# Expert weights laid out in runs of 4096 bytes, and the third weight set asked for by ScalarE behind its copy of the first gathered tokens

## The chip, the cores and the metric

The kernel runs on one core of a Trainium2 chip, as one program and one launch. The metric is the device time in microseconds (us) of one execution. Beside the times there is one profiled execution, whose trace gives every row shown below. Engines are named as in the profile: PE is TensorE (PEld its weight loads), DVE VectorE, ACT ScalarE, POOL GpSimd, SP SyncE. A "q" behind a name (SPq, ACTq) is that engine's sequencer, which also issues DMAs.

## The reference

Windowed attention (batch 8, 8 heads, 576 positions, head size 64) gives 4608 tokens of 512 numbers. A mixture of experts with a capacity follows: each token goes to the expert with the highest logit, each of the 8 experts keeps the 80 tokens of the highest gate weight, and all other rows of the output are zero.

```python
logits = x @ w_gate                                   # x: 4608 x 512 from the attention
expert_idx = np.argmax(logits, axis=1)
gate_w = probs[np.arange(N), expert_idx]
for e in range(8):
    tok_idx = ...                                     # of expert e, at most 80, highest gate_w
    h = np.maximum(x[tok_idx] @ w1[e], 0.0)           # w1[e]: 512 x 1024
    out[tok_idx] = gate_w[tok_idx, None] * (h @ w2[e])  # w2[e]: 1024 x 512
```

Each w1[e] and each w2[e] is 2 MB of float32, so one expert's set is 4 MB and all eight are 32 MB.

## The kernel before, in words

The first part, up to about 199 us, computes attention tile by tile (36 tiles of 128 tokens), writes the tokens to a DRAM buffer `x_dram`, fills the output with zeros, and works out which 80 tokens each expert keeps. The order of its instructions is a list of numbers written out by hand (`ORDER`, played by `play`). In it SP also loads the weight set of expert 0, in eight pieces of 512 KB (`first_weights`).

The second part is the experts. There are three buffers for weight sets in SBUF (`w_sets`), and expert e uses buffer e modulo 3. `weights(e)` asks for w1[e] and then w2[e] with one DMA of 2 MB each. SP asks for sets 1 and 2 at the end of the first part, and for set e+3 inside the loop once expert e has read its buffer: w1 when the last product of `ffn1(e)` is done, w2 when DVE has taken its last piece in `split(e)`.

For each expert the steps are:

- `gather(e)`: POOL issues an indirect DMA that fetches the 80 kept rows (160 KB) from `x_dram` into `xg`. All eight are issued one after the other at the start of the second part.
- `load_x(e)`: PE transposes `xg` into `tp`, and ACT copies it to `xgT` (for expert 0 ACT one half and DVE the other).
- `split(e)`: in four pieces, ACT rounds w2[e] to `wh` and DVE computes the rest `wl = w2 - wh`.
- `ffn1(e, 0)` and `ffn1(e, 4)`: PE multiplies w1[e] with `xgT` into `hp`, 64 products each; DVE turns each half into `hh` and `hl`.
- `ffn2(e)`: PE adds up three products for each of eight pieces (`hh` by `wh`, `hh` by `wl`, `hl` by `wh`) into `yp`; DVE scales the result to `y`, and POOL scatters `y` into the output with an indirect DMA.

The instructions of an engine run in the order written. For each expert the loop writes `load_x(e+1)`, `split(e+1)`, `weights(e+3)`, `ffn2(e)`, `ffn1(e+1, 0)`, `ffn1(e+1, 4)`. So on DVE the four `wl` of expert e+1 stand ahead of `y` of expert e, and that `y` stands ahead of `hh` and `hl` of expert e+1. Ahead of the first `load_x`, PE runs 24 products on idle data (L790). DMAs issued by SP are on queue q1, those by ACT on q10, and POOL's indirect ones on q0; all use the same 16 DMA engines.

Of the kernel before, what the change touches and what calls it, by code (L numbers as in the profile page):

```python
# [47 lines left out]
P = 128  # L48
# [55 lines left out]
def play(jobs, order):  # L104

    said, blocked = set(), {}
    ready = [False] * len(jobs)

    def advance(n):
        for r in jobs[n]:  # L110
            if not isinstance(r, str):
                if r[0] != "lat":
                    ready[n] = True
                    return
            elif r[0] == "!":
                said.add(r[1:])
                for m in blocked.pop(r[1:], ()):
                    advance(m)
            elif r[0] == "?" and r[1:] not in said:
                blocked.setdefault(r[1:], []).append(n)  # L120
                return

    for n in range(len(jobs)):
        advance(n)
    for n in order:
        assert ready[n], n
        ready[n] = False
        advance(n)
# [3 lines left out]
def attn_moe(ctx: ExitStack, tc: tile.TileContext, qk, v, w_gate, w1, w2, out, *, capacity, blocks, dbg=None):  # L132
    nc = tc.nc
# [3 lines left out]
    N, DM = out.shape  # L137
    E, F = w1.shape[0], w1.shape[3]
# [3 lines left out]
    KD = DM // P  # L142
# [88 lines left out]
    wp = ctx.enter_context(tc.tile_pool(name="wp", bufs=1))  # L231
    w_sets = [(wp.tile([P, KD, F], F32, name=f"w1_{i}"), wp.tile([P, KF, DM], F32, name=f"w2_{i}")) for i in range(3)]

    def weights(e):
        nc.sync.dma_start(w_sets[e % 3][0], w1[e])
        nc.sync.dma_start(w_sets[e % 3][1], w2[e])

    with ExitStack() as actx:
        ring = actx.enter_context(tc.tile_pool(name="ring", bufs=1))
# [131 lines left out]
        def first_weights(i):  # L371
            yield f"?spill{WEIGHTS_AT[i]}"
            yield "dma", 1.9
            e, i = i // NW, i % NW
            if i < KD:
                nc.sync.dma_start(w_sets[e][0][:, i], w1[e, :, i])
            else:
                c = 2 * (i - KD)
                nc.sync.dma_start(w_sets[e][1][:, c:c + 2], w2[e, :, c:c + 2])

        def tail(T):

# [302 lines left out]
        for i in range(len(WEIGHTS_AT)):  # L685
            jobs.append((2 * WEIGHTS_AT[i] + 3, first_weights(i)))
        for bi, made in enumerate(batches):
            for gi in made:
                t1 = sum(groups[gi]) - 1
# [21 lines left out]
        jobs.append((-1000, warm(False)))  # L711
        with tc.manual_schedule():
            play([gen for _, gen in jobs], ORDER)
            for e in range(1, 3):
                weights(e)

# [10 lines left out]
    def gather(e):  # L729
        xg = fk.tile([n_, DM], F32, name="xg", bufs=E)  # L730
        nc.gpsimd.indirect_dma_start(out=xg, out_offset=None, in_=x_dram[:, :],
                                     in_offset=bass.IndirectOffsetOnAxis(ap=src_i[:, e:e + 1], axis=0))
        xgs[e] = xg

    def split(e, f0, f1):
        if f0 == 0:
            wsp[e] = (wr.tile([P, KF, DM], F32R, name="wh"), wr.tile([P, KF, DM], F32R, name="wl"))
        wh, wl = wsp[e]
        for f in range(f0, f1, 2):
            nc.scalar.copy(wh[:, f:f + 2, :], w_sets[e % 3][1][:, f:f + 2, :])  # L740
            nc.vector.tensor_tensor(wl[:, f:f + 2, :], w_sets[e % 3][1][:, f:f + 2, :], wh[:, f:f + 2, :].bitcast(F32),  # L741
                                    op=ALU.subtract)

    def load_x(e):
        xTs[e] = fk.tile([P, KD, n_], F32, name="xgT")

        m = KD if e else KD // 2
        for c0 in range(0, KD, m):
            tp = ps_x.tile([P, KD, n_], F32, name="tp")
            for c in range(c0, c0 + m):  # L750
                nc.tensor.transpose(tp[:, c, :], xgs[e][:, P * c:P * (c + 1)], ident[0:n_, 0:n_])  # L751
            (nc.vector.tensor_copy if c0 else nc.scalar.copy)(xTs[e][:, c0:c0 + m], tp[:, c0:c0 + m])  # L752

    def ffn1(e, f0):
        if f0 == 0:
            hs[e] = (fk.tile([P, KF, n_], F32R, name="hh"), fk.tile([P, KF, n_], F32R, name="hl"))
        hh, hl = hs[e]
        hp = ps_h.tile([P, 4, n_], F32, name="hp")
        for f in range(4):
            for c in range(KD):  # L760
                for m in range(2):
                    col = P * (f0 + f) + 64 * m
                    nc.tensor.matmul(hp[64 * m:64 * m + 64, f, :], w_sets[e % 3][0][:, c, col:col + 64], xTs[e][:, c, :],  # L763
                                     start=(c == 0), stop=(c == KD - 1), tile_position=(0, 64 * m))
        nc.vector.tensor_scalar(hh[:, f0:f0 + 4, :], hp, 0.0, None, op0=ALU.max)
        nc.vector.scalar_tensor_tensor(hl[:, f0:f0 + 4, :], hp, 0.0, hh[:, f0:f0 + 4, :].bitcast(F32),
                                       op0=ALU.max, op1=ALU.subtract)

    def ffn2(e):
        hh, hl = hs[e]  # L770
        wh, wl = wsp[e]
        y = fk.tile([n_, DM], F32, name="y")

        w = DM if e + 1 < E else DM // 2
        for c in range(0, DM, w):
            yp = ps_y.tile([n_, DM], F32, name="yp")
            for f in range(KF):
                for i, (a, b) in enumerate(((hh, wh), (hh, wl), (hl, wh))):
                    nc.tensor.matmul(yp[:, 0:w], a[:, f, :], b[:, f, c:c + w], start=(f == 0 and i == 0),  # L779
                                     stop=(f == KF - 1 and i == 2))  # L780
            nc.vector.tensor_scalar(y[:, c:c + w], yp[:, 0:w], gw[:, e:e + 1], None, op0=ALU.mult)  # L781
        nc.gpsimd.indirect_dma_start(out=out[:, :], out_offset=bass.IndirectOffsetOnAxis(ap=dst_i[:, e:e + 1], axis=0),  # L782
                                     in_=y, in_offset=None, bounds_check=N - 1, oob_is_err=False)

    with tc.manual_schedule():
        for e in range(E):
            gather(e)
        t = ps_w.tile([P, 512], F32, name="warm")
        for _ in range(WARM2):
            nc.tensor.matmul(t[:, 0:WARMN], late, idle, start=True, stop=True)  # L790
        load_x(0)
        split(0, 0, 4)
        ffn1(0, 0)
        split(0, 4, KF)
        ffn1(0, 4)
        for e in range(E):
            if e + 1 < E:
                load_x(e + 1)
                split(e + 1, 0, KF)
            if e + 3 < E:  # L800
                weights(e + 3)
            ffn2(e)
            if e + 1 < E:
                ffn1(e + 1, 0)
                ffn1(e + 1, 4)
# [33 lines left out]
```

## Time and profile before

| | |
|---|---|
| time, median of 3 runs | 304.52 us (304.14 to 305.18) |
| profiled execution: time | 302.68 us |
| profiled execution: span, first to last instruction | 301.0 us |
| PE busy | 263.4 us, 88% of the span |
| DVE busy | 212.2 us, 71% |
| ACT busy | 140.1 us, 47% |
| moved by DMA | 84.41 MB, mean 280 GB/s |

The profiled execution took 1.84 us less than the median of the runs. Between its span and its time lie 1.68 us. A busy share is a mean over both parts, which have different limits, so the second part has to be looked at by itself.

### The profile page before, as it was taken

Reading aid. Unit: us, or ns where it says so; the run is one execution under the profiler, and the core shown is the slowest. Engines: PE = TensorE matmul, PEld = TensorE weight load, DVE = VectorE, ACT = ScalarE, POOL = GpSimd, SP = SyncE. Lnnn points to the kernel's source line nnn. Section 1 sums busy time; section 2 is a strip of 40 time slices with the busy share of each in tenths; the row PEclk is TensorE's granted clock in tenths of the full one; section 3 lists DMA queues with packets and bytes.
Section 4 is the critical chain, followed back from the end, with each engine's and each line's share of the span. In section 5 each row is a group of like instructions: output and inputs, shape, how many; then the busy total and the mean of one; then the engine's idle time right before and its main releaser. Section 6 shows DMA issues by size and latency. Waiting matters only on the chain. (4 is left out here: it accounts for less than half of the span.)

```text
span 301.0 us, 12891 instructions
## 1 busy us (share of the span) xinstructions
PE 263.4 (88%) x5616; PEld 213.2 (71%) x5616; DVE 212.2 (71%) x544; ACT 140.1 (47%) x300; POOL 137.6 (46%) x190
## 2 busy tenths in 40 slices
PE   8498899598999988979889988772999999999993
PEld 5387678486788777758877766562976887787693
DVE  0586776357889978977889999940876587667651
ACT  1475565355668565545647535101535235515500
POOL 5488577653779499636877640036010110110011
PEclk9999999879999999999999999997799999999999
DMA  7689786495877998998787849999999999998100
GB/s 266 245 294 317 226 278 168 161 283 178 277 254 240 297 302 283 307 342 285 238 286 195 311 138 301 359 435 352 334 333 365 425 433 425 425 421 356 39 24 22
DMA packets 26281, 84.41 MB, mean 280 GB/s; under 512 B 3057, under 2 KB 4209, under 8 KB 24433
## 3 DMA queue, kind: packets, MB, share of 16 engines
q1 hardware_dynamic: 25056, 80.90, 76.3%
q0 software_dynamic: 1024, 2.62, 2.6%
q8 instruction: 44, 0.72, 1.0%
q14 instruction: 13, 0.10, 0.1%
q10 hardware_dynamic: 144, 0.07, 0.1%
HBM read 63.39 MB, written 20.19 MB: 278 GB/s over the span
## 5 line engine op out<-in xcount | busy, mean ns | idle before, releaser
L285 PE MATMUL sc<-qkT 64*64 64x128 f32 x1152 | 43.7, 282 | 12.5 <-issue 8.5
L351 POOL TENSOR_TENSOR pL<-pL,keeps 128x512 f32<-128x512 f32 x36 | 45.9, 1279 | 15.3 <-ACT pL L329 12.6
L316 POOL TENSOR_TENSOR fd<-fd,mx 128x512 f32<-128x512 f32 x36 | 37.7, 1051 | 21.0 <-DVE mx L314 13.4
L285 PEld LDWEIGHTS sc<-qkT 64*64 64x64 f32 x1152 | 33.4, 137 | 19.5 <-issue 13.0
L741 DVE TENSOR_TENSOR wl<-w,wh 128x1024 fp32r<-128x1024 f32 x32 | 37.1, 1219 | 11.0 <-ACT wh L740 10.2
L782 POOL DMA_INDIRECT out_dram<-y,dst_i x8 | 7.4, 921 | 81.0 <-DVE y L781 81.0
L310 DVE COPY_PREDICATED fd<-mine,sc 128x512 f32<-128x512 int32 x36 | 26.5, 735 | 24.4 <-ACT fd L308 24.2
L401 PE MATMUL o<-vw,pL 64*64 64x65 f32 x1152 | 38.5, 225 | 2.7 <-issue 2.0
L763 PEld LDWEIGHTS hp<-xgT,w 128*64 128x64 f32 x1024 | 38.3, 143 | 3.1 <-issue 1.6
L763 PE MATMUL hp<-xgT,w 128*64 128x80 f32 x1024 | 39.6, 241 | 0.2 <-ACT xgT L752 0.2
L401 PE MATMUL o<-vw,pU 64*64 64x65 f32 x1024 | 37.2, 219 | 1.0 <-issue 1.0
L401 PEld LDWEIGHTS o<-vw,pL 64*64 64x64 f32 x1152 | 32.2, 134 | 7.7 <-issue 6.4
L308 ACT COPY fd<-sc 128x512 f32<-128x512 f32 (+1 forms) x36 | 21.1, 585 | 35.3 <-PE sc L285 35.2
L740 ACT CAST wh<-w 128x1024 fp32r<-128x1024 f32 x32 | 31.2, 1047 | 4.4 <-DMA w<-in_w_dram 4.3
L401 PEld LDWEIGHTS o<-vw,pU 64*64 64x64 f32 x1024 | 31.4, 135 | 1.4 <-issue 1.3
L752 ACT COPY xgT<-tp 128x320 f32<-128x320 f32 (+1 forms) x8 | 3.3, 410 | 51.7 <-PE tp L751 45.3
L779 PE MATMUL yp<-wh,hh 128*80 128x512 f32 (+1 forms) x72 | 26.8, 372 | 0.0
L779 PE MATMUL yp<-wl,hh 128*80 128x512 f32 (+1 forms) x72 | 26.4, 367 | 0.0
L779 PE MATMUL yp<-wh,hl 128*80 128x512 f32 (+1 forms) x72 | 26.3, 365 | 0.0
L422 PE MATMUL xT_ps<-ident,xt 128*128 128x128 f32 x144 | 23.4, 284 | 3.1 <-issue 1.7
L426 ACT COPY xT<-xT_ps 128x512 f32<-128x512 f32 x36 | 21.0, 587 | 9.6 <-PE xT_ps L422 8.9
L412 DVE TENSOR_TENSOR xt<-o,r 128x512 f32<-128x512 f32 x36 | 24.7, 686 | 0.9 <-DVE r L410 0.2
(117 smaller groups left out, 492.1 us busy)
## 6 DMA issues: line engine op xcount, KB each, us to landing
w<-in_w_dram SPq DMA_DIRECT2D x14, 2048.0 KB, 17.9
qkT<-in_qk_dram SPq DMA_DIRECT2D x32, 512.0 KB, 4.6
x_dram<-xt SPq DMA_DIRECT2D x36, 256.0 KB, 3.5
out_dram<-zeros SPq DMA_DIRECT2D x36, 256.0 KB, 4.7
vw<-in_v_dram SPq DMA_DIRECT2D x32, 260.0 KB, 4.7
w<-in_w_dram SPq DMA_DIRECT2D x8, 512.0 KB, 5.8
qkT<-in_qk_dram SPq DMA_DIRECT2D x8, 256.0 KB, 5.0
vw<-in_v_dram SPq DMA_DIRECT2D x8, 130.0 KB, 5.1
```

The lines of the kernel that those rows point to most:

```text
L285: nc.tensor.matmul(scs[T][64 * m:64 * m + 64, r, pr, :], qkT[hp, i, pr, 0, :], kw, start=True, stop=True, tile_position=(64 * r, 64 * m))
L308: nc.scalar.copy(fd[rows], sc[rows, :, :, 0:64])
L310: nc.vector.copy_predicated(fd, mine.unsqueeze(1).unsqueeze(1).broadcast_to([P, NP, 2, 64]), sc[:, :, :, 64:128])
L316: nc.gpsimd.tensor_tensor(fd, fd, mx.unsqueeze(3).broadcast_to([P, NP, 2, 64]), op=ALU.subtract)
L351: nc.gpsimd.tensor_tensor(pL, pL, keeps[:, 1:2, :].broadcast_to([P, 2 * NP, 64]), op=ALU.mult)
L401: nc.tensor.matmul(ov[64 * m:64 * m + 64, g, pr, :], pTs[T][1 - old][hp, 2 * pr + m, :], vw[hp, i - old, pr, :], start=(old == 0), stop=bo ...
L412: nc.vector.tensor_tensor(xt.rearrange("x a g d -> x g a d"), ov[:, :, :, 0:D], r.unsqueeze(3).broadcast_to([P, 2, 4, D]), op=ALU.mult)
L422: nc.tensor.transpose(tp[:, c, :], xf[:, P * c:P * (c + 1)], ident)
L740: nc.scalar.copy(wh[:, f:f + 2, :], w_sets[e % 3][1][:, f:f + 2, :])
L741: nc.vector.tensor_tensor(wl[:, f:f + 2, :], w_sets[e % 3][1][:, f:f + 2, :], wh[:, f:f + 2, :].bitcast(F32), op=ALU.subtract)
L763: nc.tensor.matmul(hp[64 * m:64 * m + 64, f, :], w_sets[e % 3][0][:, c, col:col + 64], xTs[e][:, c, :], start=(c == 0), stop=(c == KD - 1) ...
L779: nc.tensor.matmul(yp[:, 0:w], a[:, f, :], b[:, f, c:c + w], start=(f == 0 and i == 0), stop=(f == KF - 1 and i == 2))
```

## The change

The weights lie in DRAM in another order. Before, the 16 KB that one SBUF partition takes from w1[e] (or w2[e]) were contiguous, so that a 2 MB DMA was 128 runs of 16 KB. Now the array is cut in four blocks of 512 KB, and each block has 4 KB for each partition; a 2 MB DMA is 512 runs of 4 KB. The pieces of set 0, each one such block, had runs of 4 KB before and have them now, and lie contiguous as a whole. What stands in SBUF at the end is the same.

`weights` takes the engine that issues. SP asks for set 1 alone at the end of the first part. Set 2 is asked for by ACT, between `load_x(0)` and `split(0)`.

```diff
-    def weights(e):
-        nc.sync.dma_start(w_sets[e % 3][0], w1[e])
-        nc.sync.dma_start(w_sets[e % 3][1], w2[e])
+    def weights(e, eng=nc.sync):
+        t1, t2 = w_sets[e % 3]
+        eng.dma_start(t1, w1[e].rearrange("k p f -> p k f"))
+        eng.dma_start(t2.rearrange("p (k j) d -> p k j d", j=2), w2[e].rearrange("k p j d -> p k j d"))
...
             if i < KD:
-                nc.sync.dma_start(w_sets[e][0][:, i], w1[e, :, i])
+                nc.sync.dma_start(w_sets[e][0][:, i], w1[e, i])
             else:
                 c = 2 * (i - KD)
-                nc.sync.dma_start(w_sets[e][1][:, c:c + 2], w2[e, :, c:c + 2])
+                nc.sync.dma_start(w_sets[e][1][:, c:c + 2], w2[e, i - KD])
...
             play([gen for _, gen in jobs], ORDER)
-            for e in range(1, 3):
-                weights(e)
+            weights(1)
...
         load_x(0)
+        weights(2, nc.scalar)
         split(0, 0, 4)
...
-        "w1": inputs["moe_w1"].reshape(E, DM // P, P, F).transpose(0, 2, 1, 3),
-        "w2": inputs["moe_w2"].reshape(E, F // P, P, DM).transpose(0, 2, 1, 3),
+        "w1": inputs["moe_w1"].reshape(E, DM // P, P, F),
+        "w2": inputs["moe_w2"].reshape(E, F // P // 2, 2, P, DM).transpose(0, 1, 3, 2, 4),
```

On SP's queue, at the end of the first part, these instructions stood before (`w_0`, `w_1`, `w_2` are the three buffers, the numbers behind them the tile's own):

```order
L369 DMA out_dram<-zeros 128x512 x5
L235 DMA w_1_113<-in_w_dram 128x4096
L236 DMA w_1_114<-in_w_dram 128x4096
L235 DMA w_2_115<-in_w_dram 128x4096
L236 DMA w_2_116<-in_w_dram 128x4096
L235 DMA w_0_111<-in_w_dram 128x4096
L236 DMA w_0_112<-in_w_dram 128x4096
```

In the change the same place reads:

```order
L370 DMA out_dram<-zeros 128x512 x5
L236 DMA w_1_113<-in_w_dram 128x4x1024
L237 DMA w_1_114<-in_w_dram 128x4x1024
L236 DMA w_0_111<-in_w_dram 128x4x1024
L237 DMA w_0_112<-in_w_dram 128x4x1024
```

The two DMAs into buffer 2 are gone from SP, and set 3 (into buffer 0) follows set 1 there.

On ACT, where the second part begins with the copy of the first tokens, there stood before:

```order
L665 COPY wide_0_105<-vp 24x80
L555 COPY wide_2_101<-zt 24x384
L558 COPY wide_2_104<-zt 24x384
L665 COPY wide_1_106<-vp 24x80
L752 COPY xgT<-tp 128x160
L740 CAST wh<-w_0_112 128x1024 x4
```

Now there stand:

```order
L666 COPY wide_0_105<-vp 24x80
L556 COPY wide_2_101<-zt 24x384
L559 COPY wide_2_104<-zt 24x384
L666 COPY wide_1_106<-vp 24x80
L752 COPY xgT<-tp 128x160
L236 DMA w_2_115<-in_w_dram 128x4x1024
L237 DMA w_2_116<-in_w_dram 128x4x1024
L740 CAST wh<-w_0_112 128x1024 x4
```

The two DMAs stand between the copy of expert 0's tokens and the four casts of w2[0].

## Rows read from the trace of the kernel before

**Rows 1.** Page, part 2: DMA rate in 40 equal slices of the span.
```profile
GB/s 266 245 294 317 226 278 168 161 283 178 277 254 240 297 302 283 307 342 285 238 286 195 311 138 301 359 435 352 334 333 365 425 433 425 425 421 356 39 24 22
```

**Rows 2.** Waits from 190 us on: who, for whom, us in total, times, longest.
```profile
PE tp L751 <- DMA xg<-x_dram,src_i: 6.7, 1, 6.7
ACT wh L740 <- DMA w<-in_w_dram: 4.3, 5, 1.3
```

**Rows 3.** Timeline from 199 us: start, us, engine, line, operation, count, idle before.
```profile
199.25 2.79 PE L790 MATMUL warm<-idle,late 128*128 128x256 bf16 x24 [0.24 <-DVE late L586]
199.76 1.16 POOL L731 DMA_INDIRECT xg<-x_dram,src_i  x1 [23.06 <-DMA out_dram<-zeros]
...
209.35 0.29 ACT L752 COPY xgT<-tp 128x160 f32<-128x160 f32 x1 [14.31 <-PE tp L751]
209.61 3.88 ACT L740 CAST wh<-w 128x1024 fp32r<-128x1024 f32 x4
...
209.70 6.80 PE L763 MATMUL hp<-xgT,w 128*64 128x80 f32 x128 [0.16 <-ACT xgT L752]
```

**Rows 4.** Windows: busy of PE, PEld, DVE, ACT, POOL; clock, DMA share, GB/s.
```profile
3.70:4.20 0.50, 0.50 (x4) 0.38 (x3) 0.00 (x0) 0.00 (x0) 0.50 (x2) 1.00 1.03 426
206.00:208.00 2.00, 0.00 (x0) 0.00 (x0) 0.00 (x0) 0.00 (x0) 1.62 (x2) 0.85 0.98 332
214.00:216.00 2.00, 2.00 (x60) 2.00 (x58) 1.69 (x3) 0.00 (x0) 0.00 (x0) 0.94 1.08 323
196.00:204.00 8.00, 5.45 (x55) 4.26 (x53) 2.98 (x15) 0.00 (x0) 3.32 (x4) 1.00 1.05 437
206.00:228.00 22.00, 19.10 (x295) 16.26 (x296) 13.88 (x18) 8.79 (x11) 3.68 (x4) 0.84 1.01 333
232.00:274.00 42.00, 42.00 (x625) 32.94 (x624) 28.40 (x37) 16.68 (x20) 3.67 (x4) 1.00 1.01 426
```

**Rows 5.** DMA landings after issue: gathers and scatters (min/median/max), and w1[2].
```profile
DMA to landing us min/median/max: 8.9/16.5/23.8
...
DMA to landing us min/median/max: 2.6/7.6/10.5
...
w<-in_w_dram SPq DMA_DIRECT2D x1, 2048.0 KB, 23.9
```

**Rows 6.** DMA queues from 207 to 209 us, then 2 to 3: packets, MB, share.
```profile
q1 hardware_dynamic: 42, 0.54, 83.8%
q0 software_dynamic: 42, 0.12, 19.0%
...
q1 hardware_dynamic: 91, 0.19, 69.1%
q10 hardware_dynamic: 86, 0.04, 15.2%
```

**Rows 7.** Timeline of SP: issues of w1[1] and w1[2].
```profile
193.53 0.88 SPq L235 DMA_DIRECT2D w<-in_w_dram  x1
...
197.32 0.33 SPq L235 DMA_DIRECT2D w<-in_w_dram  x1
```

**Rows 8.** Timelines of ACT, DVE and PE around experts 0 and 1.
```profile
217.29 3.90 ACT L740 CAST wh<-w 128x1024 fp32r<-128x1024 f32 x4
228.82 3.90 ACT L740 CAST wh<-w 128x1024 fp32r<-128x1024 f32 x4 [0.82 <-DMA w<-in_w_dram]
...
218.41 4.62 DVE L741 TENSOR_TENSOR wl<-w,wh 128x1024 fp32r<-128x1024 f32 x4
222.95 0.74 DVE L781 TENSOR_SCALAR y<-yp,gw 80x512 f32<-80x512 f32 x1
225.41 0.49 DVE L765 TENSOR_SCALAR hh<-hp 128x320 fp32r<-128x320 f32 x1 [1.73 <-PE hp L763]
...
227.29 0.44 PE L779 MATMUL yp<-wh,hh 128*80 128x512 f32 x1
...
232.94 4.68 PE L763 MATMUL hp<-xgT,w 128*64 128x80 f32 x128
```

## Prediction

> **What bounds the kernel now.** I read the page first. Its slices of 7.5 us show the DMA rate rise to 435 GB/s where the experts begin, sink to 333 to 365 for four slices, and hold 421 to 433 for five more [rows 1]. So the experts have to be read apart from the attention, and with the DMA queues beside PE.
>
> The waits from 190 us on come next. Only two matter: PE waited 6.7 us for the first gathered tokens, and ACT waited five times, 4.3 us in all, for a w2 that was still on its way [rows 2]. The timeline shows the first wait. The 24 idle products of PE run from 199.25 to 202.04; the gather is issued at 199.76; ACT copies the transposed tokens at 209.35, and PE starts `ffn1(0)` at 209.70 [rows 3]. The gather landed 8.9 us after its issue; a scatter later in the run landed in 2.6 us at best [rows 5]. The queues show why it is slow: between 207 and 209 us q1 carries 42 packets and 0.54 MB, q0 also 42 packets but 0.12 MB [rows 6]. The two queues take turns packet by packet, and a packet of q1 is 16 KB (semaphore writes are counted too).
>
> The idle time costs PE its clock as well. The granted clock is 0.85 in the mean from 206 to 208, so it fell from 2.4 to 1.2 GHz at about 207.4, in PE's wait for the tokens; from 214 to 216 it is 0.94, so it came back at about 214.2 [rows 4]. `ffn1(0)` took 6.80 us [rows 3]; the same 128 products take 4.68 us at the full clock [rows 8], so the low clock cost 2.1 us.
>
> From expert 1 on PE is busy all the time and DMA is full too, 426 GB/s at a share of 1.01 [rows 4]. The two are close to equal: PE takes 5.65 us for `ffn2` (227.29 to 232.94) and 4.68 us for `ffn1` [rows 8], 10.3 us an expert, and a set of 4.19 MB with a scatter of 0.16 MB takes 10.2 us at 426 GB/s.
>
> **The change, part by part.**
>
> *The gather.* With 4 KB packets on q1 it waits for a quarter of the bytes at each turn. Bounds: 2.6 us (an idle DMA) and 8.9 us (nothing gained). Of the 6.3 us between, I keep a quarter: 2.6 + 1.6 = 4.2 us, so it lands at 204.0. PE's transposes, ACT's copy and DVE's half take about 1.0 us (208.7 to 209.70), so `ffn1(0)` starts at 205.0. PE has then waited 2 us, not 6.7, so I take the clock to stay at 2.4 GHz, and `ffn1(0)` ends at 209.7 instead of 216.5: a gain of 6.8 us at this place.
>
> *Set 2 on ACT.* ACT reaches its two issues at 204.9. An issue takes 0.33 to 0.88 us [rows 7]; at 0.4 each the casts of w2[0] start 0.8 us later than they could, 205.7. That delays `wl` of expert 0. DVE needs 4 x 1.16 us for `wl` (4.62 for four) and 2 x 1.0 us for `hh` and `hl`, so `ffn2(0)` starts at about 210.1, when its first `hl` is there, and ends at 216.2, and `ffn1(1)` ends at 220.9. With 0.88 for each issue it is 1 us more; the next step hides it, since w2[1] comes later still.
>
> *Where set 2 lands on the path.* This decides. At 205.3, when w2[2] has been asked for, w2[1] is not there. Before, w1[2] landed at 197.32 + 23.9 = 221.2 [rows 5, 7]. It was directly behind w2[1] on q1, and 2.1 MB at 333 GB/s [rows 4] take 6.3 us, so w2[1] landed at about 215, hidden, since ACT cast it only at 217.29 [rows 8]. In the change q10 carries set 2 beside it. At 2 to 3 us the trace has these two queues at once: 91 packets of q1 and 86 of q10 [rows 6], turn by turn. I allow 1.2 us from the issue to set 2's first packets (an estimate, under half of the 2.6 us in which the fastest scatter landed [rows 5]): 206.5. Then 8.5 us of w2[1]'s way are left, of which q1 has about 84% [rows 6], 7.1 us, and the gathers 1.4. With a q10 packet of equal size in each turn the 7.1 become 14.2: landing at 222.1. If the rate is 426 and not 333, as before and behind this stretch, everything shrinks by 426/333 = 1.28, to 12.2 us: 218.7. I take 221, nearer the slow end, since gathers are under way in most of the stretch and the slow rate came with them.
>
> The Trainium skill says the same of such queues ("DMA: Bandwidth & Descriptors", section "Queues, rings and completion order"): each DMA engine takes turns between its queue rows, packet by packet. By its section "Issuing engines are not separate DMA queues", issuing from more engines saves only issue time and the transfers interleave. The trace agrees, with 91 packets against 86. By these sections asking from ACT brings no bandwidth, and takes half of the rate from whatever SP has under way; the sum by them is the one below.
>
> *What w2[1] holds up.* Let it land at T. ACT casts, and DVE ends the four `wl` of expert 1 5.7 us later (217.29 to 223.03). Behind them on DVE stand `y` of expert 0, 0.74 us, and `hh` and `hl` of expert 1, 0.98 for the first pair [rows 8]. So `ffn2(1)` starts at T + 7.4 and ends 5.65 later, at T + 13.0. Before it ended at 232.94, set by PE. The point from which the new wait costs time is T = 219.9. With T = 221 it ends at 234.0, 1.1 us later than before.
>
> *The clock once more.* PE ends `ffn1(1)` at 220.9 and waits for `ffn2(1)` until 228.4, 7.5 us. The wait in which the clock fell before was 6.7 us, so I expect the same here, and for `ffn2(1)` the price that `ffn1(0)` paid, 2.1 us. Bounds: nothing, and half of the 5.5 us that the clock stayed low after work began (208.7 to 214.2), 2.7 us. Together: 1.1 + 2.1 = 3.2 us late.
>
> *The rest.* Experts 2 to 7 go on at PE's pace of 10.3 us, as before. The runs of 4 KB cost DMA a little: 426 GB/s at a share of 1.03 in a stretch with such packets alone, 437 at 1.05 for 16 KB and some of 2 KB, 426 at 1.01 for 16 KB later [rows 4]. At a full share that is 414 against 416 to 422, so up to 2%, 0.2 us a set or 1.4 for seven. Nothing at the end: PE comes 3.2 us later, and each set has that much more time. The pieces of set 0 keep their 4 KB packets, so the attention stays as it is.
>
> **Sum.** The gain of 6.8 us is used up before `ffn2(1)`, and 3.2 us are lost behind it: span 301.0 + 3.2 = 304.2 us, time 302.7 + 3.2 = 305.9. That execution was 1.8 us under the median of the runs, so the median comes to 304.5 + 3.2 = 307.7 us.
>
> **The rivals.**
>
> *Faster: w2[1] isn't held up.* If T stays under 215, because q1's packets go first or because w2[1] is almost down when q10 starts, the gain stays until the weights bind. ACT already waits up to 1.3 us for w2 [rows 2], so DMA would be the bound. The slow stretch would end with the gathers at about 214 instead of 228: 14 us at 333 instead of 426 are 3.1 us. 1.4 us go to the smaller packets, and about 1 us of slack in the last sets is used: 3.1 - 1.4 + 1 = 2.7 us faster, 301.8. Against it stands the even count of the two queues [rows 6]. 20%.
>
> *No change.* T near 219.9 and a clock that doesn't fall: at T = 218.7, PE waits from 220.9 to 226.1, 5.2 us, less than the 6.7 us of before, and `ffn2(1)` ends at 231.7. Then set 2, which shares its way with w1[3], is late by about as much. Within 1 us of before. 10%.
>
> *Slower by more.* The slow rate isn't tied to the gathers and holds until 228, as before: T = 222.1 or later by a larger share of gathers, say 224: `ffn2(1)` ends at 237.0 + 2.1 = 239.1, 6.2 us late, 310.7. 25%.
>
> *The gather is no sooner.* It waits for something other than packet size and lands at 208.7 again. Set 2 is then asked for at 210, 5 us of w2[1] are left at 211.2, and they double: T = 221, but PE ends `ffn1(1)` later, at about 226.5, and keeps its clock in `ffn2(1)`: 1.1 us slower, 305.6. 10%.
>
> **How the numbers follow.** My forecast, w2[1] at 219.9 to 223 and a fallen clock, has 35%, and 307.7 us is its time, 306.6 to 310.3 by its own bounds (T = 219.9 with 2.1 us for the clock, T = 223 with 2.7). The cases of less time on one side and more on the other give the range: 302.3 to 311.5. A measurement of this kernel can tell about 0.3%, 0.9 us. Faster 20%; within 0.3% the case of no change, 10%; slower 35 + 25 + 10 = 70%.
>
> **What would show it.** The first gather lands about 4 us after its issue and `ffn1(0)` takes 4.7 us at clock 1.00. ACT's casts of w2[1] wait for a DMA until about 221 (before 217.29 with no such wait). PE then has a gap of some 7 us ahead of `ffn2(1)`, and the windows show a clock under 1.00 behind it. Expert 1's `y` comes about 3 us later than before, and that distance stays to the end. It is wrong if ACT doesn't wait for w2[1], if set 2 lands behind set 1 as on one queue, or if q1 slows in the attention.

## The result, and the profile after

With the change the kernel takes 307.96 us (median of 4 runs, 307.38 to 315.02), and the kernel before on the same chip 304.85 us (median of 4, 304.14 to 310.44). The ratio is 1.0111, with a 95% interval from 1.0076 to 1.0146; disturbed executions are left out of it and of the ratios further down, but not of the medians. So the change is slower by about 1.1%. The profiled execution took 307.38 us, its span is 305.7 us.

Of the 4.7 us by which the span grew (301.0 to 305.7), 0.7 lie ahead of the second part: PE's idle products start at 199.97 us and not at 199.25 [rows 3]. Below, moments in the second part are counted from that start, so that runs can be laid over each other.

| us after the first idle product | before | change | difference |
|---|---|---|---|
| `ffn1(0)` starts | 10.45 | 7.57 | -2.9 |
| `ffn2(1)` starts | 28.0 | 25.15 | -2.9 |
| `ffn2(2)` starts | 38.6 | 40.63 | +2.0 |
| `ffn1(3)` starts | 44.2 | 48.16 | +3.9 |
| end | 101.75 | 105.73 | +4.0 |

In the kernel before, `ffn2(2)` and the `ffn1(3)` behind it stood here:

```profile
237.85 0.44 PE L779 MATMUL yp<-wh,hh 128*80 128x512 f32 x1
...
243.49 4.71 PE L763 MATMUL hp<-xgT,w 128*64 128x80 f32 x128
```

The gain is there, it is kept for two experts, and about 7 us are lost around `ffn2(2)`. The timeline of PE in the change shows it (start, us, engine, line, operation, count, idle time before it and its releaser):

```profile
199.97 2.79 PE L790 MATMUL warm<-idle,late 128*128 128x256 bf16 x24 [0.24 <-DVE late L587]
206.75 0.50 PE L751 MATMUL tp<-ident,xg 80*128 80x80 f32 x4 [3.99 <-DMA xg<-x_dram,src_i]
207.54 3.23 PE L763 MATMUL hp<-xgT,w 128*64 128x80 f32 x45 [0.29 <-ACT xgT L752]
211.17 3.12 PE L763 MATMUL hp<-xgT,w 128*64 128x80 f32 x83 [0.41 <-issue]
...
225.12 0.43 PE L779 MATMUL yp<-wh,hh 128*80 128x512 f32 x1
...
230.78 4.65 PE L763 MATMUL hp<-xgT,w 128*64 128x80 f32 x128
235.36 0.50 PE L751 MATMUL tp<-ident,xg 80*128 80x80 f32 x4
240.60 0.68 PE L779 MATMUL yp<-wh,hh 128*80 128x512 f32 x1 [4.74 <-DVE hh L765]
...
248.13 4.65 PE L763 MATMUL hp<-xgT,w 128*64 128x80 f32 x128
```

The wait for the first gathered tokens is down from 6.7 us [rows 2] to 3.99, since the first gather lands 6.2 us after its issue and not 8.9 [rows 5]:

```profile
DMA to landing us min/median/max: 6.2/8.7/8.9
```

`ffn2(1)` at 225.12 has no wait in front. `ffn2(2)` at 240.60 has 4.74 us, and takes 7.53 us up to 248.13 where 5.65 was usual [rows 8]. Its releaser is DVE's `hh`, so the wait is followed back to DVE and ACT. The timeline of ACT:

```profile
207.19 0.29 ACT L752 COPY xgT<-tp 128x160 f32<-128x160 f32 x1 [11.43 <-PE tp L751]
207.22 0.38 ACTq L236 DMA_DIRECT2D w<-in_w_dram  x1
207.64 0.52 ACTq L237 DMA_DIRECT2D w<-in_w_dram  x1
208.41 3.89 ACT L740 CAST wh<-w 128x1024 fp32r<-128x1024 f32 x4 [0.93 <-issue]
...
215.86 3.90 ACT L740 CAST wh<-w 128x1024 fp32r<-128x1024 f32 x4 [0.68 <-DMA w<-in_w_dram]
...
233.68 3.89 ACT L740 CAST wh<-w 128x1024 fp32r<-128x1024 f32 x4 [7.85 <-DMA w<-in_w_dram]
```

and of DVE:

```profile
234.76 4.63 DVE L741 TENSOR_TENSOR wl<-w,wh 128x1024 fp32r<-128x1024 f32 x4 [8.81 <-ACT wh L740]
239.31 0.74 DVE L781 TENSOR_SCALAR y<-yp,gw 80x512 f32<-80x512 f32 x1
239.97 0.48 DVE L765 TENSOR_SCALAR hh<-hp 128x320 fp32r<-128x320 f32 x1
240.49 0.49 DVE L766 SCALAR_TENSOR_TENSOR hl<-hp,hh 128x320 fp32r<-128x320 f32 x1
```

The chain is read from the bottom. `hh` of expert 2 stands behind `y` of expert 1, which stands behind the four `wl` of expert 2; those wait for ACT's casts, and ACT waited 7.85 us for w2[2]. The product of `ffn1(2)` was ready at 235.4, and DVE got to it at 239.97. The cast of w2[1] had waited 0.68 us only.

Why w2[2] came so late, the DMA queues show: packets, MB and share of each, first from 219 to 230 us, then from 230 to 233.6.

```profile
q1 hardware_dynamic: 541, 2.15, 49.0%
q10 hardware_dynamic: 539, 2.15, 48.5%
...
q1 hardware_dynamic: 312, 1.27, 87.9%
q10 hardware_dynamic: 61, 0.19, 13.6%
```

For 11 us the two queues share evenly, packet for packet. On q10 is set 2, on q1 set 3, which SP asked for at 214.33 (w1) and 215.44 (w2) and which nobody needs before expert 3. The last 0.19 MB of w2[2] trickle in after that. The landings after issue, of w1[2] and w2[2], both asked for by ACT:

```profile
w<-in_w_dram ACTq DMA_DIRECT2D x1, 2048.0 KB, 15.8
...
w<-in_w_dram ACTq DMA_DIRECT2D x1, 2048.0 KB, 26.0
```

So w1[2] is down at 207.22 + 15.8 = 223.0 and w2[2] at 207.64 + 26.0 = 233.6. What q10 still had to carry when w1[2] was down shows its row from 223 to 233 us:

```profile
q10 hardware_dynamic: 396, 1.56, 38.8%
```

A part of w2[2] had come ahead of the last packets of w1[2], so 1.56 MB were left and not 2.1. At half of the 410 GB/s that DMA carries here they would take 7.6 us and be down at 230.6 (an estimate from these rows). The other 3.0 us are a tail: from 230 on q10 has 13.6% of the time of the 16 engines, no longer half. Why the last packets of a set come so slowly no run shows.

The clock, by windows (busy time of PE, PEld, DVE, ACT, POOL; granted clock; DMA share; GB/s):

```profile
206.00:208.00 2.00, 0.96 (x12) 0.80 (x14) 0.33 (x1) 0.29 (x1) 1.40 (x2) 0.78 1.03 334
208.00:210.00 2.00, 2.00 (x36) 2.00 (x34) 0.46 (x1) 1.59 (x2) 1.69 (x2) 0.50 1.04 328
...
216.00:218.00 2.00, 2.00 (x10) 1.29 (x9) 1.39 (x2) 2.00 (x3) 0.00 (x0) 1.00 1.02 334
218.00:220.00 2.00, 2.00 (x10) 1.18 (x8) 2.00 (x3) 1.76 (x2) 0.00 (x0) 1.00 1.01 406
...
238.00:240.00 2.00, 0.00 (x0) 0.00 (x0) 2.00 (x4) 2.00 (x3) 0.00 (x0) 0.50 1.00 401
242.00:244.00 2.00, 2.00 (x6) 1.18 (x5) 2.00 (x2) 0.00 (x0) 0.00 (x0) 0.50 1.03 412
244.00:246.00 2.00, 2.00 (x9) 1.25 (x8) 2.00 (x3) 0.00 (x0) 0.00 (x0) 0.83 1.02 408
248.00:274.00 26.00, 26.00 (x443) 21.20 (x443) 16.30 (x22) 8.44 (x10) 2.72 (x3) 1.00 1.03 410
```

PE stands idle from 235.9 to 240.6, its clock is at 1.2 GHz by 238, and stays there for the first 4 us of `ffn2(2)`: that is the 1.9 us more that it takes. It also fell at the end of the shorter wait for the first tokens, at about 207.1: 0.78 in the window from 206, 0.50 in the next. From 248 on the experts go at PE's pace as before, with DMA at 410 GB/s, where it was 426 [rows 4].

### The profile page after: what moved, and what is told of

Read it like the earlier page. It is cut to its first block, busy times and chain, and to the rows that moved or that the text cites. A ratio compares the mean times of both kernels' runs of the same rounds, so it can differ in the third digit from the quotient of the medians.

```text
span 305.7 us, 12891 instructions
## 1 busy us (share of the span) xinstructions
PE 264.3 (86%) x5616; PEld 213.4 (70%) x5616; DVE 211.6 (69%) x544; ACT 139.8 (46%) x300; POOL 137.5 (45%) x190
## 5 line engine op out<-in xcount | busy, mean ns | idle before, releaser
L286 PE MATMUL sc<-qkT 64*64 64x128 f32 x1152 | 41.9, 276 | 10.2 <-issue 6.3
L286 PEld LDWEIGHTS sc<-qkT 64*64 64x64 f32 x1152 | 32.1, 133 | 16.7 <-issue 10.4
L402 PE MATMUL o<-vw,pU 64*64 64x65 f32 x1024 | 37.9, 220 | 2.7 <-issue 2.7
L779 PE MATMUL yp<-wh,hh 128*80 128x512 f32 (+1 forms) x72 | 27.6, 383 | 4.7 <-DVE hh L765 4.7
L779 PE MATMUL yp<-wl,hh 128*80 128x512 f32 (+1 forms) x72 | 27.1, 377 | 0.0
L779 PE MATMUL yp<-wh,hl 128*80 128x512 f32 (+1 forms) x72 | 27.1, 376 | 0.0
L324 PE MATMUL pT_ps<-ident,fd 128*128 128x128 f32 x144 | 23.6, 288 | 2.8 <-issue 2.0
```

What stands on the lines that cost most here:

```text
L286: nc.tensor.matmul(scs[T][64 * m:64 * m + 64, r, pr, :], qkT[hp, i, pr, 0, :], kw, start=True, stop=True, tile_position=(64 * r, 64 * m))
L324: nc.tensor.transpose(tp[:, pr].rearrange("x m q -> x (m q)"), fd[:, pr].rearrange("x r k -> x (r k)"), ident)
L402: nc.tensor.matmul(ov[64 * m:64 * m + 64, g, pr, :], pTs[T][1 - old][hp, 2 * pr + m, :], vw[hp, i - old, pr, :], start=(old == 0), stop=bo ...
```

## The experiments

Three theories of the late w2[2] stood against each other. **Turns**: set 2 on ACT's queue shares evenly with set 3 on SP's, while on one queue it would go first. **Late request**: what is asked for at 207.6 can't be there in time, by whatever queue. **Runs**: DMA is slower with runs of 4 KB, and the last sets come late.

A warning on the measure comes first. The first part ends at other moments from run to run (198.5 to 207.9 us in the profiles here), and the times scatter with it: the kernel before had medians of 303.1 to 305.4 in the groups below. Two ratios of the same kernel, the layout alone, are 1.0128 and 0.9937. The second part is steadier, 101.75 and 101.35 us in two profiles of the kernel before, so the verdicts rest on it, and that the change is slower rests on it too.

| | `ffn1(0)` starts | cast of w2[2] starts | second part | median, ratio to before |
|---|---|---|---|---|
| before | 10.45 | 29.6 | 101.75 | 304.85 |
| before again | | | 101.35 | 301.5, one run |
| change | 7.6 | 33.7 | 105.73 | 307.96, 1.0111 |
| change again | 7.7 | 35.0 | 107.13 | 310.78, one run |
| layout alone, three runs | 8.0 (first) | 25.7 (first) | 98.67, 100.02, 98.54 | 1.0128, 0.9937, 0.9993 |
| request alone | 9.95 | 36.7 | 108.64 | 1.0412 |
| request late, on SP | 7.6 | 27.0 | 99.43 | 1.006 |
| set 3 after y(0) | 7.7 | 27.5 | 101.86 | 0.9954 |
| w2[2] first | 7.8 | 25.7 | 104.95 | 1.022 |

**The layout alone.** Set 2 is asked for by SP at the end of the first part again, the runs stay at 4 KB.

```diff
-            weights(1)
+            for e in range(1, 3):
+                weights(e)
...
-        weights(2, nc.scalar)
```

> The layout alone: runs of 4 KB, but SP asks for sets 1 and 2 at the end of the first part, as before. Theory A (turns: in the change w2[2], on ScalarE's queue, shares its way with set 3, which SP asks for at 214.3 and 215.4 us, and so lands at 233.6 instead of 228.8): set 2 is ahead of set 3 on one queue again, so w2[2] lands at 226 to 228 us; the first gather lands about 6 us after its issue, as in the change, since the packets it takes turns with are 4 KB; PE has no gap at expert 2; about 2 us under the kernel before, 302 to 303 us. Theory B (late: set 2 is late because it is asked for 10 us later): the same here, 302 to 303. Theory C (runs: transfers in runs of 4 KB, 410 GB/s against 426 in the steady stretch, are what makes the weights late): every wait of ScalarE for w2 grows by some 0.4 us an expert, and the time is 306 to 308 us.

Measured: a median of 304.14 us against 303.95, ratio 1.0128 [1.0041, 1.0215], and a second part of 98.67 us, 3.1 shorter than before. The gather's landing (min, median, max), then the timelines of PE and ACT and a window of the steady stretch:

```profile
DMA to landing us min/median/max: 6.4/7.0/8.7
...
208.92 6.40 PE L764 MATMUL hp<-xgT,w 128*64 128x80 f32 x128 [0.16 <-ACT xgT L753]
```

```profile
226.67 3.90 ACT L741 CAST wh<-w 128x1024 fp32r<-128x1024 f32 x4
```

```profile
240.00:270.00 30.00, 30.00 (x463) 23.65 (x461) 20.23 (x27) 11.11 (x15) 2.73 (x3) 1.00 1.03 410
```

The first gather lands 6.4 us after its issue, with 6.2 in the change and 8.9 before [rows 5]: nearly all of the gain comes from the layout. ACT casts w2[2] without a wait for a DMA, and PE is busy all through 240 to 270 at the same 410 GB/s. So runs of 4 KB cost DMA 4% of its rate but PE nothing, and the theory of the runs falls.

**The request alone.** The kernel before with 16 KB runs, in which only the request for set 2 moves to ACT.

```diff
-            for e in range(1, 3):
-                weights(e)
+            weights(1)
...
+        weights(2, nc.scalar)
```

> The request alone: runs of 16 KB as before, but set 2 is asked for by ScalarE behind its copy of the first tokens. Theory A: the gather takes turns with 16 KB packets and lands 8 to 9 us after its issue, so the request comes at about 209.5 us; w2[2] then shares its way with set 3 and lands at 235 to 237 us, with a gap on TensorE of 6 us or more ahead of it; 309 to 312 us. Theory B: late by the 2 us by which the request is later than in the change, 308 to 310 us. Theory C: with runs of 16 KB the weights are on time, 303 to 305 us.

Measured: 313.67 us, ratio 1.0412 [1.0214, 1.0609], the second part 108.64, 6.9 longer than before. From the timelines of ACT and PE:

```profile
240.09 3.89 ACT L739 CAST wh<-w 128x1024 fp32r<-128x1024 f32 x4 [8.77 <-DMA w<-in_w_dram]
```

```profile
247.00 0.68 PE L778 MATMUL yp<-wh,hh 128*80 128x512 f32 x1 [5.68 <-DVE hh L764]
```

It is the wait of the change, at the same place, with runs of 16 KB. With the layout alone at -1.7 to -3.2 us and the request at +6.9, the two add up to +3.7 to +5.2; the change has +4.0, and +5.4 when it was run again.

**The request as late, but on SP.** In the changed kernel SP asks for set 2, behind a DMA of 64 bytes that reads the copy of the first tokens, so at the moment at which ACT would.

```diff
+    mark = dram.tile([1, 16], F32, name="mark")
...
-        weights(2, nc.scalar)
+        nc.sync.dma_start(mark, xTs[0][0:1, 0, 0:16])
+        weights(2)
```

> The change, but SP asks for set 2, at the same time as ScalarE does in the change: a DMA of 64 bytes of the copied tokens to a scratch row in DRAM stands ahead of it on SP, so that SP waits for ScalarE's copy. Set 2 is then ahead of set 3 on one queue. Theory A: w2[2] lands at 224 to 228 us, TensorE has no gap at expert 2, 301 to 303.5 us. Theory B: the request is as late as in the change, w2[2] lands at 232 to 234 us, 307 to 308 us. Theory C: 306 to 308 us.

Measured: 302.66 us, ratio 1.006 [1.0008, 1.0112], the second part 99.43. The timeline of SP shows w2[2] asked for 8.3 us after the first idle product (at 201.87 in this run), where the change had 7.7, and that of ACT when it was there:

```profile
210.18 0.50 SPq L239 DMA_DIRECT2D w<-in_w_dram  x1
215.54 0.37 SPq L238 DMA_DIRECT2D w<-in_w_dram  x1
216.64 3.38 SPq L239 DMA_DIRECT2D w<-in_w_dram  x1
```

```profile
228.91 3.89 ACT L742 CAST wh<-w 128x1024 fp32r<-128x1024 f32 x4 [1.97 <-DMA w<-in_w_dram]
```

Asked for no sooner, w2[2] is cast 27.0 us after the first idle product, 6.7 sooner than in the change, because set 3 now stands behind it on the same queue. PE waits 1.3 us in the rest of the run. This is the run that tells the theories apart: the late request falls, and the turns remain.

**Set 3 later.** Set 2 stays on ACT; SP asks for set 3 only when y(0) is written.

```diff
-            if e + 3 < E:
+            if 0 < e < E - 3:
                 weights(e + 3)
...
+            if e == 0:
+                nc.sync.dma_start(mark, ys[0][0:1, 0:16])
+                weights(3)
```

> The change, ScalarE asking for set 2 as in it, but SP asks for set 3 only when the output of expert 0 has been scaled, at about 222.5 us instead of 214.3 (a DMA of 64 bytes of that output to a scratch row stands ahead of it). Theory A: set 2 has the DMA engines to itself behind set 1 and lands at 222 to 226 us; no gap at expert 2; 301 to 304 us unless set 3 in its turn is late, by at most 2 us. Theory B: w2[2] still lands at 232 us or later, 307 to 308 us. Theory C: 307 us or more, since nothing is asked for earlier.

Measured: 300.57 us, ratio 0.9954 [0.988, 1.0029], the second part 101.86. The timeline of ACT around w2[1] and w2[2], then two windows:

```profile
218.96 3.89 ACT L742 CAST wh<-w 128x1024 fp32r<-128x1024 f32 x4 [5.11 <-DMA w<-in_w_dram]
...
226.72 3.89 ACT L742 CAST wh<-w 128x1024 fp32r<-128x1024 f32 x4 [2.31 <-DVE hh L767]
```

```profile
224.00:226.00 2.00, 0.12 (x1) 0.15 (x2) 1.97 (x4) 0.41 (x1) 0.39 (x1) 1.00 0.26 104
226.00:228.00 2.00, 2.00 (x7) 1.11 (x7) 1.35 (x4) 1.28 (x2) 0.57 (x1) 0.73 0.59 92
```

Without set 3 beside it w2[2] keeps nobody waiting: the 6 to 7 us are gone, as the turns would have it. But in this run w2[1] was late, by 5.11 us, and PE waited for `ffn2(1)`:

```profile
225.88 0.43 PE L782 MATMUL yp<-wh,hh 128*80 128x512 f32 x1 [1.97 <-DVE hh L767]
...
233.10 4.65 PE L765 MATMUL hp<-xgT,w 128*64 128x80 f32 x128
```

Behind the wait of 1.97 us the clock fell, to 0.73 in the window from 226, and `ffn2(1)` took 7.2 us and not 5.65. There the gain is spent: `ffn1(2)` starts 33.86 us after the first idle product, and 33.69 before. Between set 2 and set 3 DMA is almost idle, 104 and 92 GB/s, but that costs PE nothing: it has no further wait, and the sum is even with the kernel before.

**The order of the two halves.** ACT asks for w2[2] first, then for w1[2].

```diff
-        weights(2, nc.scalar)
+        u1, u2 = w_sets[2]
+        nc.scalar.dma_start(u2.rearrange("p (k j) d -> p k j d", j=2), w2[2].rearrange("k p j d -> p k j d"))
+        nc.scalar.dma_start(u1, w1[2].rearrange("k p f -> p k f"))
```

> The change with ScalarE's two requests the other way round: w2[2], then w1[2]. Theory A (set 2 takes turns with set 3, and of its halves the one asked for second lands some 33 to 35 us after the first idle product): now w2[2] lands at about 23 us, before ScalarE wants it at 25.8, and w1[2] at about 33.7. TensorE could start its products with w1[2] at 30.8, so it waits about 3 us there instead of 4.7 to 5.9 us ahead of the second products of expert 1, and the clock falls less or not at all: second part 101 to 103.5 us (105.7 and 107.1 in the change). If what held w2[2] up in the change was not its place behind w1[2], ScalarE waits for it as before, and the second part is 105 to 107 us.

Measured: 307.44 us, ratio 1.022 [1.007, 1.0369], the second part 104.95. That is 0.8 us shorter than the change and not the gain that was expected. ACT casts w2[2] at 25.7 and waits for no DMA. The timeline of PE:

```profile
234.28 6.29 PE L763 MATMUL hp<-xgT,w 128*64 128x80 f32 x128 [4.68 <-DMA w<-in_w_dram]
```

Now PE waits 4.68 us for w1[2], and the clock falls to 0.62 and 0.52 in the two windows of 2 us from 234. Whichever half is asked for second is late, and by about as much. That fits the turns again, and shows that the order of the halves is no way out.

**Again, for the spread.** The kernel before and the change were run and profiled once more, and the layout alone twice more.

> The kernel before once more, for the spread of its second part, counted from TensorE's first idle product of it (the one ahead of expert 0's transposes) to the end of the span: 101.8 us in the profile shown of it, 101 to 103 us expected. If it is over 104 or under 100 us, a single profile can't tell the parts of the change apart.

> The change once more. Its second part was 105.7 us. Theory A (turns): w2[2] lands some 33 us after the first idle product again (27 to 30 where set 2 stands ahead of set 3 on one queue), TensorE waits about 5 us for it, second part 104.5 to 107 us. If the late w2[2] was a chance of one execution, the second part is 99 to 102 us. Set 2 can hold up w2[1] instead (it waited 0.7 us in the change and 5.1 us where set 3 was asked for later), which costs TensorE at most 2 us.

> The layout alone once more. Second part 98 to 100 us (98.7 before), no wait of ScalarE for w2. If the first part ends as early in the mean as that of the kernel before, the time is 2 to 3 us under before; if the layout of set 0 or the next set's transfers make the first part longer, the time stays within 1 us of before although the second part is shorter.

> The layout alone a third time, since its two timings leave its sign open (304.14 us beside 303.95 of before, 303.33 beside 305.43). Its second part was 98.7 and 100.0 us where that of before was 101.8 and 101.4, so 1.4 to 3.1 us faster is expected, if the first part of both kernels is the same in the mean; 98 to 100.5 us for the second part.

Measured: 101.35 us for the second part of the kernel before, 107.13 for the change, with PE waiting 5.93 us at `ffn2(2)` and the cast of w2[2] 9.03, and 100.02 and 98.54 for the layout alone. The order of the three holds. The times of the layout alone are 303.33 us, ratio 0.9937 [0.9883, 0.9991], and 302.48, ratio 0.9993 [0.994, 1.0045]: that it makes the second part 2 to 3 us shorter is in the profiles, that it makes the kernel faster the times don't show.

**More idle products.** The layout alone with 58 in place of 24 idle products ahead of the first tokens, so that PE doesn't stand idle there.

```diff
-WARM2 = 24
+WARM2 = 58
```

> The layout alone, with 58 idle products of TensorE ahead of the first tokens instead of 24, so that it works until about 6.8 us after the first of them, where the tokens land at about 7.0. If the idle time is what lowers the clock there, it stays at 1.00, the first products of expert 0 take 4.7 us instead of 6.4, and the second part is 97 to 98 us, 1 to 1.7 us under the layout alone (VectorE then sets when the second products start). If the clock falls for another reason, no change against the layout alone.

Measured: 307.25 us, ratio 1.0035 [0.998, 1.0091], so no gain. The second part took 103.13 us. The wait for the tokens was down to 0.42 us, but PE stood idle all the same, just behind it. The profile can't be laid over the others: the clock was at 0.5 to 0.6 from 196 to 206 us already, ahead of the edit, the first part ended at 207.9, and the 4.27 us of PE's idle time ahead of `ffn1(0)` are put down to no releaser. What full clock in `ffn1(0)` is worth stays open.

## Why the prediction was right, and where it was not

Direction and size were right: 307.7 us forecast, 307.96 measured, 3.2 us later forecast and 3.1 measured. The mechanism was right in kind, a set on ACT's queue that shares its way with a set on SP's. The place was not, so the sum came out right from terms that were not the real ones, and that it came so close is luck. By its own signs the place was wrong: ACT waited 0.68 us for w2[1], until 215.86 and not until 221, and PE's gap was not ahead of `ffn2(1)`. What came true, within 1 us, is the condition of the first rival, that w2[1] is almost down when q10 starts; that rival came to 2.7 us faster, because it did not count set 2 against set 3.

- **The gather** was to land 4.2 us after its issue, and landed after 6.2. I took a quarter of all that exceeds 2.6 us. In fact a part is fixed: the first packets of the gather moved 4.3 us after its issue (200.49 to about 204.8), and 4.3 us before too (199.76 to about 204.0). What the packet size shortens is the rest, 4.6 us before and 1.9 now, and that to 0.41 of it, not to a quarter.
- **`ffn1(0)`** started 7.57 us after the first idle product, where I had 5.75 (205.0 less 199.25), and its clock was not kept. PE waited 3.99 us and the clock fell all the same. Of the 6.8 us of gain I counted, 2.9 came. The cost of 0.8 us for the two issues on ACT was right: 0.38 and 0.52, and the casts start 0.93 us behind the copy.
- **Where set 2 lands on the path** is the step that failed. I had w2[1] land at 221, and it landed at about 215.9, hidden. Two terms were too small. ACT asked at 207.2 to 207.6 and not at 204.9 to 205.3. And I allowed 1.2 us from the request to q10's first packets, which moved at 210.3, 3.1 us after it. By then some 0.15 MB of w2[1] were left, not the 8.5 us of its way that the sum doubles. A third error works the other way: the share of 84% that q1 was to have beside the gathers was read with packets of 16 KB, and with 4 KB it had 68.0% from 207 to 209 us. The wait for w2[1] exists, though: in the run with set 3 later it is 5.11 us.
- **Set 2 against set 3** I had named, in a half sentence of the case of no change ("set 2, which shares its way with w1[3], is late by about as much"), and had not worked out. It decides. Even turns from 223.0 on give 230.6 for w2[2]; measured 233.6, the rest by the tail of its last packets, which no term of mine had.
- **What a late w2 holds up** was right in its terms, one expert later: `ffn2` starts at T + 7.4 by the prediction, and 233.6 + 7.0 = 240.6 in the trace.
- **The clock behind the wait** was put at 2.1 us; `ffn2(2)` took 7.53 us for 5.65, so 1.9.
- **The rest**: PE's pace held, and the smaller runs cost 4% of the DMA rate, not up to 2%, and nothing on the path.

So by the trace -2.9 us from the gather, then 4.9 lost in the wait at `ffn2(2)` and 1.9 by the clock: +3.9 at `ffn1(3)` and +4.0 at the end. The 0.7 us of the first part are no more than it varies by.

Of the section "Queues, rings and completion order" in "DMA: Bandwidth & Descriptors" of the Trainium skill, by which each DMA engine takes turns between its queue rows, this case's trace shows the price: 541 packets of q1 against 539 of q10. What I drew from it was right; I applied it only to the set that was under way when ACT asked, and not to the one that was asked for next.

Not settled: why the cast of w2[1] waited 5.11 us with set 3 later, and 0.68 and 1.54 in the two profiles of the change. ACT asked 7.3 to 7.4 us after the first idle product in all three. SP had asked for w2[1] 2.8 us ahead of the idle products there and 3.8 and 3.5 in the change, which the turns would make some 2 us of the 3.8 by which the cast is later than in the change, counted from those products. The rest is a tail again: in that run q1 moves only 24 packets, 0.08 MB, in the 5.9 us from 212.2 to 218.1, and w2[1] counts as landed with the last of them. Nor is it settled whether the layout alone is worth its 2 to 3 us in the time of the whole kernel.

## What to carry to other kernels

In these runs two queues on a full link shared it evenly, whatever was needed first, and the last packets of a shared transfer came slower still. A transfer that is needed first should stand ahead on the same queue, or the other queue should be empty for as long as it takes. When a request moves to another queue, follow it against every transfer that will be under way until it lands, those that are asked for later too, and not only against what is there when it starts. And when a wait at the start of a chain gets shorter, look which transfer further on had its cover from it.

## What the runs showed of the hardware

The first packets of the first gather came 4.3 us after its issue in both kernels, though the packets beside it were 16 KB in one and 4 KB in the other.

DMA is slow while the eight gathers are under way, at a share of 1.00 to 1.06 all the same: 275 to 334 GB/s in the windows of 2 us from 206 to 218, and 406 from 218 on, which is when the last gather lands. Before, where the last gather was issued at 208.50 and landed 23.8 us later [rows 5], at 232.3, the rate was 324 GB/s from 226 to 229 and 397 from 229 to 232, so it rose some 2 us ahead of that landing. With shorter gathers the slow stretch ends some 12 us sooner; I had left it open in two of the rivals. That the gathers cause it is read from these two ends, no run had them taken out.

With the layout of 4 KB runs a steady stretch carries 410 GB/s, with 16 KB 426 [rows 4].
